# Attention regrouped by head parity, float32 array pieces for scores and fused weights, and a first weight kept whole on the chip

## The chip, the cores and the metric

The kernel runs on one core of one Trainium2 chip. The metric is the device time of one execution in microseconds (us): 1509.26 is the median of three runs before the change (1509.16 to 1510.17). A profile was taken of one execution; its span is 1507.8 us. Engines are named as in the profile: PE is TensorE (products), PEld its weight loads, DVE is VectorE, ACT is ScalarE, POOL is GpSimd, SP is SyncE (which here only issues transfers).

## What is computed

Eight batches of eight heads attend over 576 positions through 32 "packed" queries, and the result goes through two dense layers with a gate, twice (4608 tokens, width 512, inner width 2048).

```python
# q, k, v: (8, 8, 576, 64); p: (8, 8, 32, 64); weights arrive as float64
def sm_attn(qq, kk, vv):
    s = scale * np.matmul(qq, kk.transpose(0, 1, 3, 2))
    a = np.exp(s - np.max(s, axis=-1, keepdims=True))
    a = a / (np.sum(a, axis=-1, keepdims=True) + 1e-09)
    return np.matmul(a, vv)
p_packed = sm_attn(p, k, v)                 # (8, 8, 32, 64)
out = sm_attn(q, p_packed, p_packed)        # (8, 8, 576, 64)
x = out.transpose(0, 2, 1, 3).reshape(4608, 512)
h = x @ w_in;  x = (h * sigmoid(h)) @ w_out                      # first MLP
h = x @ w_in2; x = (h * clip(h + 3, 0, 6) / 6) @ w_out2          # second MLP
```

## The kernel before

**Blocks.** The tokens go through the first MLP in nine blocks of 512. Blocks 0 to 7 are the first 512 positions of batches 0 to 7; block 8 collects the eight tails of 64 positions. In each block (`block`, L1027) a loop over f = 0 to 15 makes 128 hidden rows (`hidden`, L978), applies silu (L1001), splits the result into a high and a low float32r part (`split_g`, L1005) and, two steps later, adds it into four output banks (`project`, L1012). Every product of two values is three float32r products (high x high, high x low, low x high).

**Thin and fat blocks.** Blocks 0 and 8 are fat: `hidden` multiplies all 512 rows of x by the first weight, four chunks x three products. For block 0, x is made by `a_x` (L1674). Blocks 1 to 7 are thin: since x is (softmax weights) x (packed values), the packed values are multiplied into the first weight beforehand (`fuse_steps`, L673), in four groups g of 512 columns, and `hidden` multiplies the fused weight by the softmax weights, two chunks x three products. Batch 1 is fused alone; batches 2 and 3, 4 and 5, 6 and 7 share their products (`mates`, L636). Each product there is three float32r products of 128 rows by 128 columns, 512 wide (L682 to L684), whose operand is loaded from DRAM, where block 0 stored it (`w1i`, `keep`, `next_in`).

**Attention.** Heads are worked on in half batches of four. A score step (`step_zs`, L518) makes, for each pair of heads, one float32 product of 128 rows (two heads of 64, zeros elsewhere) by 64 columns: L528 for the packed queries against k, L524 for q against the packed values, and 64-wide tails (L537, L533). The packed values come from L482 (128 rows by 32 columns, 64 wide). k and q of batches 0 and 1 are turned on PE (L449), later ones on DVE. The k side of a batch runs one block ahead of its q side.

**Order.** All engine queues are in order and the program writes their order by hand. Before block 0 a listed prologue works through batch 0 in two halves. Inside the blocks a planner (`Plan`, L765) puts attention and fusing steps between products: each step has a place in the block, needed steps with a delay counted in products, and a number of PSUM banks, out of a ring of four that `hidden` uses too. A step whose key is "exps" is only run in a calm place (L795). `boundary` (L1942) finishes what the next block needs.

**First weights.** They arrive as pairs of 32-bit words. A unit (`conv_a` to `conv_lo`) is two ACT passes, two DVE passes and a POOL addition (L208), then a cast to the high part on ACT (L219) and a subtraction on DVE (L224). `Feed` (L1449) does two units per f in block 0, loading them on ACT's queue (L155), and stores the results on SP's queue. From block 1 on, `Prep` converts the second MLP's weights with one step per call, and `Second` (L1102) is the second MLP, seven products instead of eight, from block 8's end on.

Of the kernel before, what the change touches and what calls it, by code (L numbers as in the profile page):

```python
# [8 lines left out]
F32 = mybir.dt.float32  # L9
# [9 lines left out]
def tile_pack_attention_two_mlps(ctx: ExitStack, tc, q, k, v, p, w_in1, w_out1, w_in2, w_out2, out):  # L19

# [9 lines left out]
    HQ = P // NP  # L37
    QPB = H // HQ
    NQ = B * QPB
# [5 lines left out]
    RAW = 4  # L45
    assert TAIL * B == T and HQ * D == 2 * P and NP == 32

# [9 lines left out]
    xp = opened(first_left, "xp")  # L57
    gp = opened(first_left, "gp", bufs=3)
    wp = opened(first_right, "wp", side="right")
    at = opened(first_right, "at", side="right")  # L60
    win0 = opened(first_block, "win0", side="right", bufs=3)
# [7 lines left out]
    mask = const.tile([P, HQ, 1], F32, name="mask")  # L69
    nc.vector.memset(mask, 0.0)  # L70
    for h in range(HQ):
        nc.vector.memset(mask[h * NP:(h + 1) * NP, h, :], 1.0)
    twos = const.tile([P, 2, 1], F32, name="twos")
    nc.vector.memset(twos, 0.0)
    for h in range(HQ):
        nc.vector.memset(twos[h * NP:(h + 1) * NP, h % 2, :], 1.0)
    tails = const.tile([P, 2 * TAIL], F32, name="tails")
    nc.vector.memset(tails, 0.0)
    half = const.tile([P, 1], F32, name="half")
    nc.vector.memset(half, 0.5)  # L80
    d1s, d2s = {}, {}
# [8 lines left out]
    early, busy, other = [True], [True], [False]  # L90
    load_queue = [nc.sync]
    banks = [(ps_h, "h"), (ps_h, "h"), (ps_acc, "acc0"), (ps_acc, "acc1"), (ps_h, "h"), (ps_h, "h"), (ps_acc, "acc2")]
    spare = [(wts, f, n) for f in range(0, NF, 2) for n in range(2)] + [(xp, f"xf{c}", 0) for c in range(KC)]
# [10 lines left out]
    def spare_row():  # L104
        return gp.tile([P, 2, T], F32, tag="x1", name="spare", bufs=2).rearrange("p a t -> p (a t)")[:, 0:S]

    def copy(out, in_):
        (nc.vector.tensor_copy if other[0] else nc.scalar.copy)(out=out, in_=in_)

    def copy_short(out, in_):  # L110
        (nc.scalar.copy if busy[0] and not other[0] else nc.vector.tensor_copy)(out=out, in_=in_)

    def vec(step, *args):

        other[0] = True
        step(*args)
        other[0] = False

    def half_kb(n, tag, bufs=1, what=""):

        if n == 1 or (n == 0 and what == "q"):
            pool, tag, n = spare.pop()
            if pool is xp:
                return pool.tile([P, T], F32, tag=tag, name="spare")
            if tag not in shared:
                shared[tag] = pool.tile([P, 2, T], F32, tag=f"wr{tag}", name="spare")
            return shared[tag][:, n]
        return at.tile([P, T], F32, tag=tag, name=tag, bufs=bufs)

# [4 lines left out]
    w1i = [dram.tile([KC, P, 2, GF, P], F32, name=f"w1i{g}", tag=f"w1i{g}") for g in range(NG)]  # L136
# [6 lines left out]
    def half_w(kind, f):  # L143
        if kind == "in":
            return win0.tile([P, 2, DM], F32R, tag="win", name="win")
        if f % 2 == 0:
            return wts.tile([P, 2, DM], F32R, tag=f"wr{f}", name=f"wr{f}")
        return gp.tile([P, 2, DM], F32R, tag="wo", name="wo", bufs=WO)

    def load_raw(key, src):  # L150
        if key[0] == "in":
            raw = wp.tile([P, 2 * T], I32, tag="raw", name="raw", bufs=RAW)
        else:
            raw = win0.tile([P, 2 * T], I32, tag="raw2", name="raw2")
        (load_queue[0] if early[0] else nc.scalar).dma_start(out=raw.rearrange("p (a f) -> p a f", a=src.shape[1]), in_=src)  # L155
        raws[key] = raw
# [7 lines left out]
    def load_win(w, f):  # L164
        load_raw(("in", f), win_src(w, f))

    def load_wout(w, f):
        load_raw(("out", f), wout_src(w, f))


# [3 lines left out]
    def ring():  # L174
        return wp.tile([P, T], F32, tag="ring", name="cr", bufs=8)
# [1822 lines left out]
```

## Time and profile before

| | us |
|---|---|
| median of three runs | 1509.26 |
| span of the profiled execution | 1507.8 |
| PE busy | 1483.1 (98%) |
| DVE busy | 1036.0 (69%) |
| ACT busy | 779.4 (52%) |
| POOL busy | 192.5 (13%) |
| moved by DMA | 358.52 MB, mean 238 GB/s |

The span begins with the program's first instruction and ends with its last; 1.5 us of the median lie around it. Busy time is the union of an engine's instructions. Matmul records overlap (each is shown until its modelled end), so what a product costs is read from the distance between starts, not from its length. A stage is cut out by its start and end in us from the span's start.

### The profile page before, as it was taken

The page shows a single profiled execution, that of the slowest core. Times are in us where ns is not written, and L with a number is a line of the kernel's source. Part 1 is how long each engine was busy: PE and PEld are TensorE (multiplying, and loading weights), DVE is VectorE, ACT ScalarE, POOL GpSimd, SP SyncE. Part 2 cuts the span into 40 slices and gives each one's busy share as a digit, 9 for nine tenths or more (in the row PEclk, how much of TensorE's full clock was granted, in tenths as well). Part 3 has the DMA queues.
Part 4 walks back from the last instruction along what each step waited for, and adds up shares of the span by engine and source line. Part 5 has one row for each costly group of instructions (what it writes and reads, how often), then busy time and mean ns, then how long its engine had stood idle before and what let it go on. Part 6 is the DMA issues. An engine that isn't in the chain of part 4 may idle for free.

```text
span 1507.8 us, 21726 instructions
## 1 busy us (share of the span) xinstructions
PE 1483.1 (98%) x7550; PEld 1230.3 (82%) x7550; DVE 1036.0 (69%) x1695; ACT 779.4 (52%) x1241; POOL 192.5 (13%) x177
## 2 busy tenths in 40 slices
PE   7999999999999999999999999999999999999998
PEld 4777777777777778788878888888888888999998
DVE  6767466756575656653463779786978687778767
ACT  6876657655566456655452344334433443444443
POOL 2433011111211211123240000000000000000000
PEclk9999999999999999999999999999999999999999
DMA  9999789997698769868895576678667866997987
GB/s 246 306 306 276 247 214 253 274 253 198 177 245 263 199 165 306 231 178 239 243 291 178 193 225 216 195 216 252 219 193 223 242 215 210 286 313 255 271 273 226
DMA packets 434509, 358.52 MB, mean 238 GB/s; under 512 B 191200, under 2 KB 325856, under 8 KB 434400
## 3 DMA queue, kind: packets, MB, share of 16 engines
q1 hardware_dynamic: 422832, 343.59, 77.6%
q10 hardware_dynamic: 11568, 13.54, 2.9%
q8 instruction: 61, 1.00, 0.3%
q14 instruction: 48, 0.39, 0.1%
HBM read 295.17 MB, written 61.87 MB: 237 GB/s over the span
## 4 chain that ended last, share of the span: by engine, by line
PE 84%; ACT 6%; DMA 4%; DVE 3%; SPq 2%; issue 1%; POOL 1%; ACTq 0%; POOLq 0%; DVEq 0%
PE b L1270 8%; PE b L1268 8%; PE b L1269 8%; PE b L1363 8%; PE b L1366 7%; PE b L1365 7%; PE acc L1016 7%; PE acc L1017 7%; PE acc L1018 7%; PE hps L992 4%; PE hps L993 4%; PE hps L994 4%; DMA wo<-w1o 1%; DMA praw<-in_moe_w_out_dram 1%; PE abank L524 1%
## 5 line engine op out<-in xcount | busy, mean ns | idle before, releaser
L1009 DVE TENSOR_TENSOR gl<-hps,gh 128x512 fp32r<-128x512 f32 x144 | 98.9, 687 | 190.6 <-ACT gh L1008 187.8
L1366 PE MATMUL b<-ro,ws 128*128 128x512 f32 (+2 forms) x564 | 206.4, 366 | 0.0
L1365 PE MATMUL b<-ro,ws 128*128 128x512 f32 (+2 forms) x564 | 206.3, 366 | 0.0
L1268 PE MATMUL b<-xc,ws 128*128 128x512 f32 (+1 forms) x560 | 205.7, 367 | 0.0
L1270 PE MATMUL b<-xc,ws 128*128 128x512 f32 (+1 forms) x560 | 205.7, 367 | 0.0
L1269 PE MATMUL b<-xc,ws 128*128 128x512 f32 (+1 forms) x560 | 205.7, 367 | 0.0
L1311 DVE TENSOR_TENSOR ro<-g,ro 128x1024 fp32r<-128x1024 f32 (+1 forms) x140 | 161.5, 1158 | 41.5 <-ACT ro L1306 41.2
L1306 ACT CAST ro<-g 128x1024 fp32r<-128x1024 f32 (+1 forms) x140 | 132.0, 967 | 93.4 <-DVE g L1299 34.5
L1001 ACT ACTIVATE hps<-hps 128x512 f32<-128x512 f32 x144 | 83.9, 583 | 116.0 <-PE hps L994 115.0
L1363 PE MATMUL b<-ro,ws 128*128 128x512 f32 (+2 forms) x564 | 138.9, 367 | 0.3
L1366 PEld LDWEIGHTS b<-ro,ws 128*128 128x128 f32 x564 | 105.9, 188 | 13.1
L1365 PEld LDWEIGHTS b<-ro,ws 128*128 128x128 f32 x564 | 105.9, 188 | 13.1
L1268 PEld LDWEIGHTS b<-xc,ws 128*128 128x128 f32 x560 | 105.1, 188 | 13.2
L1269 PEld LDWEIGHTS b<-xc,ws 128*128 128x128 f32 x560 | 105.1, 188 | 13.2
L1016 PE MATMUL acc<-gh,wo 128*128 128x512 f32 x288 | 114.6, 398 | 1.3 <-DMA wo<-w1o 1.3
L1270 PEld LDWEIGHTS b<-xc,ws 128*128 128x128 f32 x560 | 105.1, 188 | 13.0
L1363 PEld LDWEIGHTS b<-ro,ws 128*128 128x128 f32 x564 | 102.9, 188 | 15.0 <-DVE ro L1311 2.1
L1016 PE MATMUL acc<-gh,wr 128*128 128x512 f32 x288 | 114.0, 396 | 0.5 <-ACT gh L1008 0.5
L1017 PE MATMUL acc<-gl,wr 128*128 128x512 f32 x288 | 112.5, 391 | 0.2 <-DVE gl L1009 0.2
L1018 PE MATMUL acc<-gh,wr 128*128 128x512 f32 x288 | 112.5, 390 | 0.0
L1018 PE MATMUL acc<-gh,wo 128*128 128x512 f32 x288 | 112.4, 390 | 0.0
L1017 PE MATMUL acc<-gl,wo 128*128 128x512 f32 x288 | 112.4, 390 | 0.0
(310 smaller groups left out, 2899.4 us busy)
## 6 DMA issues: line engine op xcount, KB each, us to landing
ws<-w2in SPq DMA_DIRECT2D x280, 256.0 KB, 3.3
ws<-w2out SPq DMA_DIRECT2D x280, 256.0 KB, 3.5
wi<-w1i SPq DMA_DIRECT2D x80, 512.0 KB, 6.6
wo<-w1o SPq DMA_DIRECT2D x64, 512.0 KB, 6.2
x1d<-x SPq DMA_DIRECT2D x18, 512.0 KB, 5.2
w1i<-win SPq DMA_DIRECT2D x16, 512.0 KB, 7.2
praw<-in_moe_w_in_dram SPq DMA_DIRECT2D x32, 256.0 KB, 6.2
praw<-in_moe_w_out_dram SPq DMA_DIRECT2D x32, 256.0 KB, 5.7
```

Source lines behind the costliest of these rows:

```text
L1009: nc.vector.tensor_sub(out=gl, in0=g, in1=f32(gh))
L1016: mm(acc[e], lhsT=w[:, 0, s], rhs=gh, start=first, stop=False)
L1017: mm(acc[e], lhsT=w[:, 0, s], rhs=gl, start=False, stop=False)
L1018: mm(acc[e], lhsT=w[:, 1, s], rhs=gh, start=False, stop=last)
L1268: mm(ps, lhsT=wh, rhs=xs[k][:, 0, c], start=first, stop=False, skip_group_check=True)
L1269: mm(ps, lhsT=wh, rhs=xs[k][:, 1, c], start=False, stop=False, skip_group_check=True)
L1270: mm(ps, lhsT=wl, rhs=xs[k][:, 0, c], start=False, stop=last, skip_group_check=True)
L1306: nc.scalar.copy(out=t[:, 0], in_=v)
L1311: nc.vector.tensor_sub(out=t[:, 1], in0=self.operand(s), in1=f32(t[:, 0]))
L1363: mm(to, lhsT=wh, rhs=x, start=False, stop=last, skip_group_check=True)
L1365: mm(to, lhsT=wh, rhs=x, start=first, stop=False, skip_group_check=True)
L1366: mm(to, lhsT=wl, rhs=x, start=False, stop=False, skip_group_check=True)
```

## The change

- A batch is worked on whole. A tile has the four even heads of a batch on one side and the four odd heads on the other: rows e x 64 of a turned tile belong to parity e, and columns c x 32 to head pair c. One softmax tile (`soft`) of 128 x 1152 replaces two of 128 x 576.
- A score step is eight float32 products of 64 rows by 32 columns, 512 wide (`scores_of`), written pair by pair, even then odd; the even ones go to one bank and the odd ones to another. The tails are four products of 128 rows by 32 columns, 128 wide.
- The first weight is converted to plain float32 and kept on the chip (`wi`, four tiles); it is no longer split or stored for fusing. A fusing step is eight such float32 products per group and block (`fuse_products`); its two banks are then split into high and low parts (`fuse_split`). Batches are not paired any more.
- Block 0 is thin too: its g = 0 is fused in the prologue, g = 1 to 3 in the block. `a_x` and its splits go. The prologue works on all eight heads at once and converts four units before block 0.
- Attention of batch j + 1 runs wholly inside block j, with g = 0 of its fusing at 0.88 of the block.
- Block 8's first weight is stored once from `wi` in block 1 (`w1s`), loaded in 16 pieces of 256 KB and split on the chip (`win_load`, `win_split`).
- The planner's class is as it was but for `finish`; the keys of the exponentials are now "exps0", "exps1", "exps20", "exps21".

```diff
-    w1i = [dram.tile([KC, P, 2, GF, P], F32, name=f"w1i{g}", tag=f"w1i{g}") for g in range(NG)]
+    wi = [at.tile([P, KC, T], F32, tag=f"wi{g}", name=f"wi{g}") for g in range(NG)]
+    w1s = [dram.tile([P, KC, GF, P], F32, name=f"w1s{g}", tag=f"w1s{g}") for g in range(NG)]
...
     def conv_add(key):
         r, t = raws.pop(key)
+        if key[0] == "in":
+            nc.gpsimd.tensor_add(out=wi[key[1]][:, key[2], :].bitcast(I32), in0=r, in1=t)
+            return
         nc.gpsimd.tensor_add(out=r, in0=r, in1=t)
...
+    def win_load(f):
+        lo, hi = (fr.tile([P, KC, P], F32R, tag="fused", name="win", bufs=12) for _ in range(2))
+        nc.sync.dma_start(out=f32(lo), in_=w1s[f // GF][:, :, f % GF, :])
+        have_in[f] = hi, lo
+    def win_split(f):
+        hi, lo = have_in[f]
+        nc.scalar.copy(out=hi, in_=f32(lo))
+        nc.vector.tensor_sub(out=lo, in0=f32(lo), in1=f32(hi))
...
+    def scores_of(c, lhs, turned, to):
+        for e in range(2):
+            rows = slice(e * D, (e + 1) * D)
+            mm(to[e][c * NP:(c + 1) * NP, :], lhsT=lhs[rows, c * NP:(c + 1) * NP], rhs=turned[rows, :], start=True, stop=True)
+    def scores_tail(what, lhs):
+        to, dg = bank(), spread_tails[what]
+        for c in range(HP):
+            mm(to[c * NP:(c + 1) * NP, 0:2 * TAIL], lhsT=lhs[:, c * NP:(c + 1) * NP], rhs=dg[:, c].rearrange("p e t -> p (e t)"), start=True, stop=True)
+        return to
...
+    def fuse_products(b, g):
+        to, t = (bank(), bank()), st["ppT", b]
+        for c in range(KC):
+            scores_of(c, t, wi[g][:, c, :], to)
+        return to
+    def fuse_split(b, g, to):
+        made_ = []
+        for e in range(2):
+            hi, lo = (fr.tile([P, T], F32R, tag="fused", name="fused", bufs=12) for _ in range(2))
+            nc.scalar.copy(out=hi, in_=to[e])
+            made_.append((hi, lo))
+        for e, (hi, lo) in enumerate(made_):
+            nc.vector.tensor_sub(out=lo, in0=to[e], in1=f32(hi))
+            fused[b, g, e] = hi, lo
...
+    def attention(b):
+        first = b < 2
+        add("kp", 0.0, 3, lambda: step_small(b), bank=7)
...
+        add("s", 0.17, 6, lambda: step_s(b), ("kp", 7), (last, 7), bank=9, count=3)
...
+        for e in range(2):
+            add(f"max{e}", 0.17, 0, lambda e=e: max1(b, e), ("s", 5 + 3 * e))
+            add(f"exps{e}", 0.17, 0, lambda e=e: exp1(b, e), (f"max{e}", 6))
+        add("t", 0.3, 6, lambda: step_t(b), ("exps1", 10), bank=8, count=3)
+        add("pp", 0.4, 9, lambda: step_pp(b), ("t", 9), ("post1", 0), bank=6)
+        add("pt", 0.45, 3, lambda: step_pt(b), ("pp", 7), bank=7)
+        add("z", 0.52, 6, lambda: step_z(b), ("pt", 8), (last, 7), bank=12, count=3)
...
+        add("m0", 0.88, 4, lambda: fuse(b, 0), ("pt", 9), bank=15, count=2)
...
     def hidden(j, f, tick, nxt):
-        if j in (0, B):
+        if j == B:
...
+    for _ in range(4):
+        feed.load()
...
+    to = fuse_products(0, 0)
+    ub = operand_u(0, 1)
+    fuse_split(0, 0, to)
...
+                plan.add(("m", j, g), lo + (hi - lo) * (0.6 if j else 0.9), 4, lambda g=g: fuse(j, g), bank=15, count=2)
```

## Rows read from the trace of the kernel before

**Rows 1.** The page's first part: busy us, share of the span, instructions

```profile
PE 1483.1 (98%) x7550; PEld 1230.3 (82%) x7550; DVE 1036.0 (69%) x1695; ACT 779.4 (52%) x1241; POOL 192.5 (13%) x177
```

**Rows 2.** Busy time by stage; columns as in the fence's first line

```profile
core 0: us, PE busy (x) PEld busy (x) DVE busy (x) ACT busy (x) POOL busy (x), PEclk, DMA share, GB/s
0.00:36.70 36.70, 27.90 (x196) 17.09 (x197) 22.44 (x58) 22.45 (x44) 8.22 (x15) 0.92 1.01 245
36.70:152.70 116.00, 110.67 (x573) 85.42 (x572) 84.08 (x151) 87.28 (x160) 45.58 (x38) 0.96 0.98 298
152.70:252.00 99.30, 95.69 (x590) 72.45 (x589) 59.10 (x128) 58.62 (x97) 13.84 (x17) 1.00 0.81 220
...
500.00:578.30 78.30, 78.30 (x441) 61.58 (x440) 46.22 (x103) 46.32 (x80) 15.58 (x16) 1.00 0.76 200
578.30:656.80 78.50, 78.49 (x350) 62.37 (x349) 52.62 (x99) 47.79 (x78) 12.02 (x10) 1.00 0.76 225
656.80:722.30 65.50, 65.50 (x291) 54.29 (x290) 28.69 (x57) 35.61 (x62) 21.76 (x18) 1.00 0.84 222
722.30:811.00 88.70, 87.98 (x387) 72.29 (x386) 39.09 (x64) 38.99 (x64) 23.55 (x17) 1.00 0.86 252
```

**Rows 3.** Timeline of PE in block 7: start us, length us, line, tiles, shape

```profile
656.77 0.39 PE L992 MATMUL hps<-a2h,xf 128*128 128x512 f32 x1
...
658.81 0.39 PE L992 MATMUL hps<-a2h,xf 128*128 128x512 f32 x1
```

**Rows 4.** Groups by line, PE, fusing: count, busy us, mean ns

```profile
L682 PE MATMUL abank<-wi,ph 128*128 128x512 f32 x64 | 25.9, 404 | 0.0
```

**Rows 5.** Timeline of PE in block 5, one score step of a half batch

```profile
544.16 1.08 PE L524 MATMUL abank<-T,ppT 128*64 128x512 f32 x4
545.07 1.03 PE L528 MATMUL abank<-T,kp 128*64 128x512 f32 x4
545.93 0.28 PE L533 MATMUL abank<-qtT,ppT 128*64 128x64 f32 x4
...
546.26 0.65 PE L482 MATMUL abank<-nat,T 128*32 128x64 f32 x32
546.84 0.32 PE L485 MATMUL abank<-vt,a1Tt 64*32 64x64 f32 x8
```

**Rows 6.** Timeline of PE in block 0, into and out of a score step

```profile
53.63 0.39 PE L994 MATMUL hps<-xh,win 128*128 128x512 f32 x1
53.95 1.08 PE L528 MATMUL abank<-T,kp 128*64 128x512 f32 x4
...
55.08 0.50 PE L1016 MATMUL acc<-gh,wo 128*128 128x512 f32 x1
55.41 0.40 PE L1017 MATMUL acc<-gl,wo 128*128 128x512 f32 x1
```

**Rows 7.** DMA issues: tiles, queue, count, KB each, median us to landing

```profile
wi<-w1i SPq DMA_DIRECT2D x80, 512.0 KB, 6.6
w1i<-win SPq DMA_DIRECT2D x16, 512.0 KB, 7.2
raw<-in_moe_w_out_dram ACTq DMA_DIRECT2D x13, 512.0 KB, 6.3
```

**Rows 8.** Timeline of ACT's queue in block 0: one issue of a load

```profile
42.01 0.42 ACTq L155 DMA_DIRECT2D raw<-in_moe_w_in_dram  x1
```

**Rows 9.** Groups by line in block 0: count, busy us, mean ns, idle before

```profile
L219 ACT CAST win<-cr 128x512 fp32r<-128x512 f32 x14 | 8.7, 620 | 11.9 <-POOL cr L208 10.6 <-DMA w1i<-win 1.1
L467 ACT ACT_TABLE_LOAD x2 | 2.6, 1283 | 0.0
L224 DVE TENSOR_TENSOR win<-cr,win 128x512 fp32r<-128x512 f32 x14 | 13.7, 980 | 11.1 <-ACT win L219 10.9
L208 POOL TENSOR_TENSOR cr<-cr 128x512 int32<-128x512 int32 x30 | 42.4, 1432 | 61.7 <-DVE cr L199 55.6 <-ACT gh L1008 6.1
```

**Rows 10.** Timeline of DVE in the prologue: a maximum over 576 columns

```profile
22.51 0.75 DVE L1639 TENSOR_REDUCE s2m<-d 128x18 f32<-128x576 f32 x1
```

## What to expect, worked out before the run

> **What bounds the kernel now.** I read the page's busy line first. TensorE (PE) is busy 98% of the span and VectorE (DVE) and ScalarE (ACT) 69% and 52% [rows 1], so the time should come from what PE is given, wherever PE does not wait. To see where that holds I cut the span at the first hidden-layer product of each token block and read the busy time of the stages [rows 2]. A plain block is 16 x 18 = 288 products of 512 columns. Block 7 is almost nothing else: its products start 0.2267 us apart (ten starts, nine steps, in 2.04 us [rows 3]), and 288 x 0.2267 = 65.3 us against its 65.5 us. Everything above 65.5 us in the other thin blocks is therefore attention, fusing or waiting:
>
> - blocks 2 to 6 take 404.8 us together (252.0 to 656.8 [rows 2]), 77.3 us above five plain blocks;
> - block 1 takes 99.3 us, 33.8 above plain;
> - block 0 has 384 products (87.1 us) and takes 116.0 us;
> - the prologue takes 36.7 us.
>
> In block 0 the other engines tell more than PE: ACT is busy 87.3 of 116 us, DMA stands at 0.98 of its 16 engines with 298 GB/s, and PE's granted clock averages 0.96 of 2.4 GHz. There ACT, DVE and DMA set the pace together, not PE alone [rows 2]. The second MLP, from 811 us on, is not touched: 0.
>
> **Block 0's hidden layer.** It goes from 12 to 6 products per f: 96 fewer, 96 x 0.2267 = 21.8 us less PE work.
>
> **Fusing.** Before, blocks 1 to 7 have 192 fused products (three groups of 64 such as the one in [rows 4]), 192 x 0.2267 = 43.5 us: 12 for each pair and group, 48 for block 1 alone. After, each of eight blocks has four steps of eight float32 pieces (64 rows by 32 columns, 512 wide). What such a step costs is the number on which all hangs. The trace shows a pair of float32 pieces of 128 rows by 64 columns: each piece leaves two records, and four records pass in 545.07 - 544.16 = 0.91 us, the next four in 0.86 [rows 5]. It also shows four pieces side by side: 32 records of 128 rows by 32 columns, 64 wide, pass in 546.84 - 546.26 = 0.58 us. Sixteen pieces one after another, at an eighth of 0.86 us each, would be 1.72 us, and still 0.86 if the pieces of a pair ran in turn too. So column groups do run together. No row has two row groups at once. Bounds for a step: 0.86 us (all eight together) and 8 x 0.86 = 6.9 us (one after another), with 1.7 us between if the two row groups take turns. I take 0.91: the eight pieces lie on eight different places of the array, as the four do in the row, their outputs go to two banks, and rows 0 to 63 and rows 64 to 127 read different partitions. The Trainium skill ("TensorEngine Tiling (Array Packing)", sections Tiling Modes and Restrictions and Gotchas) lists 64x32 as eight independent tiles whose row tiles must write different PSUM banks; by that rule the step is near the lower bound, and no run here has shown it yet. The same page says that a change of tiling mode drains the engine, which speaks against many short steps. The rows have that price: the last product before such a step is followed after 53.95 - 53.63 = 0.32 us and the first behind it after 55.41 - 55.08 = 0.33 instead of 0.23 [rows 6], so about 0.2 us, with the drain behind the last piece some 0.3. One fusing step: 0.91 + 0.3 = 1.2 us. Four a block: 4.8 us, and 3.6 in block 7, whose first group is made in block 6.
>
> **Attention on PE, per batch.** Before, block 5 (78.3 us [rows 2]) has 12.8 us above plain; 12 fused products are 2.7, so a batch costs 10.1 us. Of that the change alters three terms. Four pairs of scores, 4 x 0.885 = 3.5 us, become two steps of eight pieces, 2 x 0.91 = 1.8: -1.7. The tail scores, 546.26 - 545.93 = 0.33 us for each half batch [rows 5] and so 0.66, become two sets of four pieces of 128 columns, a quarter of 0.91 and some fill each, 0.5: -0.2. One transpose of p and one of packed values go: -0.2. The packed values (0.58 us for each half in [rows 5]), the turned weights and the tail outputs are as many as before, and so, about, are the entries and exits. After: 8.0 us. Nothing is removed from the softmax itself: its elements are the same, in one tile of 1152 columns instead of two of 576. A steady block is then 65.5 + 8.0 + 4.8 = 78.3, and I add 0.3 for waits of the kind that remain: 78.6. The splits of the fused tiles fall from 16 half-height pairs per block to 8 full-height ones on ACT and DVE, which are busy 46 of 78 us there [rows 2]: hidden, worth nothing by itself. The 80 reads of first weights of 0.5 MB each [rows 7] become 16 of half the size; DMA is at 0.76 in blocks 5 and 6, so this is hidden too.
>
> - Blocks 2 to 6: 5 x 78.6 = 393.0 against 404.8: -11.8.
> - Block 1: 78.6, plus 3 for late loads of the kind it has now; 81.6 against 99.3: -17.7. Its 48 fused products and the half batch that ran ahead go.
> - Block 7: 65.5 + 3.6: +3.6.
> - Block 8: same 384 products. Its 16 first weights are now loaded in one piece and split on the chip, 16 x about 0.6 us on ACT and 0.7 on DVE (a cast and a subtraction of 512 columns), beside 39 us of either in 88.7 us [rows 2]: hidden. Only the first ones stand at the boundary, behind the splits of x: +0.5.
>
> **Block 0.** PE's own sum: 65.5 + 8.0 + 4.8 + 32 transposes of batch 1's k and q (about 4) = 82 us. ACT's sum decides. It has 87.3 us busy now and issues 24 raw loads on its queue (13 in [rows 7], the other 11 of the same kind) at some 0.44 us [rows 8], 10.6 us; the rest of the 116 us is waiting, 10.6 us of it for GpSimd (POOL) in the casts of first-weight tiles alone [rows 9]. The change takes away 14 such casts (8.7 us) and with them that wait, and on DVE the 14 subtractions (13.7 us) [rows 9]. About half the turned k and q tiles go to DVE (-3). It adds six more splits of fused tiles (6 x 0.6 = 3.6) and, I think, two more table loads at 1.28 (2.6 [rows 9]): the planner's rule that an exponential runs only in the calm place behind a silu asks for a step named "exps", and the steps are now "exps0", "exps20" and so on, so exponentials fall where they like. ACT: 87.3 - 8.7 - 3 + 3.6 + 2.6 = 81.8 busy, 26 issues are 11.4, sum 93. With 2 us of waiting 95. ACT's queue is in order, so the product's silu and split stand behind each late cast. PE alone would allow 82; block 0 at its present pace of 116 us is the other end. I take 95: -21. DMA must keep up: 298 GB/s x 116 us = 34.6 MB now; without the 16 stores of first weights of 0.52 MB [rows 7] (8.4 MB) and some five early reads of them (2.6 MB) 23.6 MB are left, 79 us at the same rate. That cover is thin.
>
> **Prologue.** Block 0 now needs all of batch 0, and four converted units, before its first product, where before half a batch after the other could pass. Ahead of the last q piece in the queue are k, v, q (3.5 MB), p and two units of 0.52 MB: 4.6 MB, at 245 GB/s [rows 2] 19 us, plus some 2.5 until data flow: 21.5. Then packing, turning and the scores, 3 us, and DVE's queue: two long and one short piece through transpose, maximum, subtraction, sum and scaling at about 0.7 us each (576 columns take 0.75 [rows 10]), three units' bits at 1.1: 10.7 us, to 35; then two operand transposes and their splits, with the fused split between, 4 us: 39.5. The gain of 12 small products is inside that. Against 36.7: +2.8.
>
> **Sum.** +2.8 - 21.0 - 17.7 - 11.8 + 3.6 + 0.5 = -43.6. The profiled execution's span is 1507.8 us and the median of the runs 1509.26, so 1.5 us lie around the span. 1507.8 - 43.6 + 1.5 = 1465.7, say 1466 us.
>
> **The rivals.** What can be told from no change is about 0.2%, 3 us.
>
> - *The row groups take turns.* Seven batches in blocks have 14 score steps, fusing has 32, the prologue at least 1: 47 steps. If the even and the odd half each run as one group, every step costs 0.86 more: +40 us, 1506. For it: no row shows two row groups together. Against it: the pieces share neither rows, banks nor partitions. 4%.
> - *Slower: every piece waits for the one before.* The pieces are written even head, odd head, next pair, so if row groups exclude each other and PE keeps that order, no two pieces overlap: 47 x 7 x 0.86 = +283 us, 1749. It makes the kernel slower from about 43.6 / 47 = 0.93 us extra per step on, a little over one more turn. 6%.
> - *Block 0 keeps its pace.* ACT, POOL and DVE are chained in order through each converted unit; if POOL's additions (1.43 us each [rows 9]) or DMA set the pace, block 0 stays near 112 to 116 and the prologue ends 3 us later: about 1489. For it: DMA at 0.98 now. Against it: the waits listed are mostly for first-weight casts, which go. 15%.
> - *The softmax chain shows.* A whole batch now runs within one block, with shorter planned delays, three of the four h banks taken at once by a score step, and exponentials with table loads between silus. If PE waits 3 us per block in seven blocks: 1487. 13%.
> - *Block 0 runs at PE's own sum* (82 us): 1453. 10%.
> - *The forecast*, 1466, its own range 1456 to 1478: 52%.
>
> The range 1447 to 1492 holds all but the first two and some tails, about 8 in 10. Faster by over 0.2%: 0.91; within 0.2%: 0.03; slower: 0.06.
>
> **What would show it.** The spacing from the first record of a score or fusing step to the first record behind it: 0.9 to 1.2 us if right, 1.7 or 7 if a rival holds. Block 7 at 69 us is the cleanest place, since it has three fusing steps and nothing else. Block 5 should stay near 78, block 1 stand near 82, block 0 near 95 with ACT close to full and its first product near 39.5 us, and the second MLP should not move. Wrong it would be if blocks 2 to 6 grow (PE idle before steps that follow exponentials), or if block 0's DMA share stays at 0.98 with units arriving late.

## The result, and the profile after

The changed kernel takes 1518.17 us (median of three runs, 1516.45 to 1518.56) against 1509.26: a ratio of 1.0051 with a 95% interval of 1.0031 to 1.0070. It is slower by about 8 us, where 1466 was forecast. The span of its profiled execution, the fastest of the three, is 1514.7 us, 6.9 above that of before. The page's busy line, as [rows 1]: PE is busy 28 us less than before.

```profile
PE 1454.8 (96%) x7860; PEld 1167.6 (77%) x7860; DVE 1011.8 (67%) x1590; ACT 736.0 (49%) x1146; POOL 187.3 (12%) x150
```

Busy time by stage, cut and with columns as in [rows 2]: prologue, blocks 0 and 1, then 3, 6 and 7.

```profile
0.00:43.00 43.00, 26.44 (x204) 12.26 (x204) 22.94 (x48) 16.64 (x31) 7.84 (x13) 0.91 0.84 206
43.00:172.90 129.90, 98.65 (x540) 67.49 (x541) 81.75 (x149) 84.19 (x140) 42.22 (x30) 0.87 0.57 168
172.90:257.70 84.80, 81.41 (x505) 59.05 (x504) 47.09 (x89) 42.33 (x70) 11.77 (x10) 0.98 0.74 209
338.10:417.60 79.50, 79.50 (x505) 58.10 (x504) 47.08 (x93) 43.22 (x72) 13.96 (x12) 1.00 0.64 169
577.80:659.50 81.70, 79.94 (x506) 58.21 (x505) 47.79 (x95) 42.29 (x70) 13.04 (x11) 1.00 0.56 152
659.50:729.50 70.00, 70.00 (x337) 54.33 (x336) 31.11 (x62) 40.09 (x71) 21.84 (x18) 1.00 0.86 234
```

| stage | before | after | forecast of the difference | measured |
|---|---|---|---|---|
| prologue | 36.7 | 43.0 | +2.8 | +6.3 |
| block 0 | 116.0 | 129.9 | -21.0 | +13.9 |
| block 1 | 99.3 | 84.8 | -17.7 | -14.5 |
| blocks 2 to 6 | 404.8 | 401.8 | -11.8 | -3.0 |
| block 7 | 65.5 | 70.0 | +3.6 | +4.5 |
| block 8 | 88.7 | 87.5 | +0.5 | -1.2 |
| second MLP | 696.8 | 697.7 | 0 | +0.9 |

From block 1 on the change gains 13 us. Block 0 and the prologue cost 20. In block 0 ACT is busy about as long as forecast (84.2 us for 81.8) and DVE 81.8 us, DMA has become free (0.57 of its engines against 0.98 in [rows 2]), and yet 130 us pass. What PE waited for in block 0 (waited for, total, times, longest), of before and then of after:

```profile
PE abank L449 <- DVE gl L1009: 4.6, 2, 2.3
PE hps L992 <- DVE gl L1009: 0.6, 1, 0.6
```

```profile
PE abank L567 <- POOL tails L560: 11.0, 1, 11.0
PE acc L829 <- ACT wr L184: 8.0, 1, 8.0
PE hps L802 <- ACT fused L590: 7.3, 3, 3.8
PE abank L406 <- DVE gl L822: 2.6, 1, 2.6
```

Before, PE waits only 5.2 us in all of block 0, but that does not make the other queues slack. The trace's chain (from the last instruction back to what released each one, as far as the profile can infer it) runs through PE for 48 of that block's 116 us. From 37.0 to 74.3 us and from 88.2 to 118.5 it runs through ACT, DVE, POOL and transfers, and PE's two waits of 2.3 us for `gl` stand where these two stretches end. So PE's work and the chain beside it were about equally long. Ends of the second stretch (start us, us, what):

```profile
88.01 0.14 PE abank L537 x4
88.15 1.12 SPq L382
...
117.15 0.59 ACT gh L1008
117.77 0.70 DVE gl L1009
118.51 0.55 PE abank L449 x3
```

After, PE waits over 30 us, and its granted clock averages 0.87 of 2.4 GHz. PE's own sum is about 83.5 us (block 3's 79.5 with no waits, and some 4 for 32 more transposes), so 46 us of block 0 are waits and what follows from them: PE stands for 31 us (129.90 - 98.65), and its work takes some 15 us longer. Part of the 15 is the clock. From 56.1 to 62.9 us, a stretch that begins while PE stands in its wait of 8.0 (51.8 to 59.7 us), the granted clock is 0.50, which is 1.2 GHz, and products start 0.42 us apart (61.19, 61.61); behind it they start 0.23 apart (63.37, 63.60). Some 30 such distances in the block make 7 us; the other 8 were not traced. The stretch by busy time, its clock third from the end:

```profile
56.10:62.90 6.80, 3.16 (x9) 2.45 (x10) 3.83 (x8) 3.78 (x8) 1.07 (x1) 0.50 0.83 291
```

The other queues show where PE's waits begin. DVE's and ACT's longest waits in block 0 of after:

```profile
DVE gl L822 <- ACT gh L821: 34.0, 15, 5.4
```

```profile
ACT cr L142 <- DVE cr L161: 9.9, 7, 2.4
ACT wr L184 <- POOL cr L173: 9.0, 5, 3.8
ACT a2h L540 <- DVE abank L535: 7.9, 2, 4.5
ACT cr L142 <- DMA raw<-in_moe_w_out_dram: 4.5, 2, 4.2
```

DVE stands at `gl` (the low half of a hidden tile) until ACT has made `gh`; ACT stands at a conversion pass or at a cast until DVE's bit passes (L157, L161) or POOL's addition behind them are done. They work in turn rather than side by side. ACT's timeline at the start of the block (start us, us, line, operation, tiles, idle before) shows one such turn, the one behind PE's 8.0:

```profile
46.64 1.28 ACT L510 ACT_TABLE_LOAD   x1
47.94 0.31 ACT L510 ACTIVATE soft<-soft 128x128 f32<-128x128 f32 x1
48.26 1.28 ACT L814 ACT_TABLE_LOAD   x1
...
54.97 0.67 ACT L142 ACTIVATE cr<-raw 128x512 f32<-128x512 f32 x1 [4.21 <-DMA raw<-in_moe_w_out_dram]
...
59.07 0.62 ACT L184 CAST wr<-cr 128x512 fp32r<-128x512 f32 x1 [0.34 <-issue]
```

The cast at 59.07 is second-weight unit 0, for which PE's first output product waits. A table load and an exponential for batch 0's 128 tail columns stand ahead of the block's first silu, and a conversion whose load is late stands ahead of the cast.

### The profile page after: what moved, and what is told of

Same layout as the page of the kernel before. It is cut to its first block, busy times and chain, and to the rows that moved or that the text cites. A ratio compares the mean times of both kernels' runs of the same rounds, so it can differ in the third digit from the quotient of the medians.

```text
span 1514.7 us, 21753 instructions
## 1 busy us (share of the span) xinstructions
PE 1454.8 (96%) x7860; PEld 1167.6 (77%) x7860; DVE 1011.8 (67%) x1590; ACT 736.0 (49%) x1146; POOL 187.3 (12%) x150
## 4 chain that ended last, share of the span: by engine, by line
PE 86%; ACT 5%; DVE 4%; DMA 2%; issue 1%; POOL 1%; SPq 1%; ACTq 0%; POOLq 0%; DVEq 0%
PE acc L829 8%; PE b L1087 8%; PE b L1085 8%; PE b L1086 8%; PE b L1180 8%; PE b L1183 7%; PE acc L831 7%; PE b L1182 7%; PE acc L830 7%; PE hps L802 4%; PE hps L804 4%; PE hps L803 4%; PE abank L406 3%; DMA nat<-in_k_dram 1%; ACT hps L814 1%
## 5 line engine op out<-in xcount | busy, mean ns | idle before, releaser
L829 PE MATMUL acc<-gh,wr 128*128 128x512 f32 x288 | 117.0, 406 | 8.0 <-ACT wr L184 8.0
L829 PE MATMUL acc<-gh,wo 128*128 128x512 f32 x288 | 117.2, 407 | 3.1 <-DMA wo<-w1o 3.0
L802 PE MATMUL hps<-a2h,fused 128*128 128x512 f32 x256 | 107.0, 418 | 7.3 <-ACT fused L590 7.3
L831 PE MATMUL acc<-gh,wo 128*128 128x512 f32 x288 | 114.0, 396 | 0.1
L831 PE MATMUL acc<-gh,wr 128*128 128x512 f32 x288 | 113.5, 394 | 0.4 <-DVE wr L189 0.4
```

What stands on the lines that cost most here:

```text
L802: mm(ps, lhsT=wh, rhs=rh, start=c == 0, stop=False)
L829: mm(acc[e], lhsT=w[:, 0, s], rhs=gh, start=first, stop=False)
L831: mm(acc[e], lhsT=w[:, 1, s], rhs=gh, start=False, stop=last)
```

## Experiments

Block 0 is cut by its first hidden products, as above. The prologue, whose program is the same in most kernels, ends between 42.8 and 45.7 us, so single spans scatter by a few us. Ratios are to the kernel before, on the same chip.

| run | block 0 | ratio (95%) |
|---|---|---|
| changed kernel | 129.9 | 1.0051 (1.0031 to 1.0070) |
| e1_twice | 139.7 | 1.0130 (1.0113 to 1.0146) |
| e2_less_conv | 118.4 | 0.9961 (0.9946 to 0.9976) |
| e3_tails_late | 128.4 | 1.0047 (1.0029 to 1.0065) |
| e4_loads_early | 127.3 | 1.0053 (1.0034 to 1.0072) |
| e5_bits_early | 136.7 | 1.0099 (1.0074 to 1.0124) |
| e6_plan_brisk | 132.1 | 1.0064 (1.0041 to 1.0087) |
| e7_fuse_early | 154.2 | 1.0219 (1.0195 to 1.0243) |
| e8_together | 134.6 | 1.0069 (1.0051 to 1.0087) |
| e9_no_soft | 123.5 | 1.0009 (0.9999 to 1.0019) |
| e10_no_add | 115.8 | 0.9955 (0.9938 to 0.9973) |
| e11_both | 106.0 | 0.9871 (0.9849 to 0.9894) |
| e12_calm | 130.5 | 1.0108 (1.0090 to 1.0126) |
| e13_start | 125.0 | 1.0038 (1.0023 to 1.0053) |
| e14_low_on_pool | 135.4 | 1.0084 (1.0067 to 1.0101) |
| e15_start_pool | 125.3 | 1.0018 (1.0009 to 1.0028) |
| e16_cover | 135.6 | 1.0092 (1.0076 to 1.0107) |
| e17_cover_pool | 140.5 | 1.0111 (1.0093 to 1.0128) |
| e18_bits_ahead | 113.3 | 0.9949 (0.9934 to 0.9963) |

### Is it the PE work that is gone?

```diff
+        if j == 0:
+            for c, (wh, wl, rh, rl) in enumerate(parts):
+                mm(ps, lhsT=wh, rhs=rh, start=c == 0, stop=False)
...
```

> The changed kernel, with each of block 0's 96 hidden-layer products made twice (the second set starts its sum anew, so the values are the same): 96 x 0.2267 = 21.8 us more PE work in block 0, nothing more for any other engine. Theory (the queues of ACT, DVE and POOL set block 0's pace and PE waits for them): block 0 grows by 0 to 8 us, from 129.9 to at most 138, because the products fill waits; the time stays within 1516 to 1526 us. Rival (PE's own work sets the pace): block 0 grows by about 22 us, to 152, and the time to 1540.

It fell between the two: +9.8 us, so over half of the 21.8 us went into waits that were there anyway, and the rest added. More to the point, with PE's load back at 12 products per f block 0 takes 139.7 us where the kernel before takes 116. So the block is not long because PE's cover is gone; the chain beside PE became slower.

### How much of it is load on ACT, DVE and POOL?

Work is left out: conversion passes (`conv_b`, `conv_shift`, `conv_sign` for units converted inside block 0), POOL's additions too, batch 1's softmax passes, and conversion passes and softmax together.

```diff
+        if not early[0] and key[0] != "p":
+            raws[key] = raw[:, :, 1], r, r
+            return
...
-            add(f"exps{e}", 0.17, 0, lambda e=e: exp1(b, e), (f"max{e}", 6))
+            add(f"exps{e}", 0.17, 0, lambda e=e: b == 1 or exp1(b, e), (f"max{e}", 6))
...
```

> The changed kernel, with part of the computation left out: for the units converted inside block 0, one of the two ACT passes (26 of 0.65 us) and both DVE passes (28 units, 0.4 + 0.7 us) are not made; loads, POOL additions, casts and subtractions stay. Theory (the conversion in the in-order queues sets block 0's pace): ACT loses some 15 us and DVE some 28 us of block 0's work, and block 0 falls by 20 to 40 us, to 90 to 110 us. Rival (PE's own work or the float32 pieces set the pace): block 0 stays within 5 us of 129.9. If the loads of raw weights are what is late, it also stays above 120, since they are all still there.

> As the run with fewer conversion passes, and POOL's additions left out too: in block 0 a unit is one ACT pass, then the cast and the subtraction of the second weight; the low bits of these weights are missing. Run with fewer passes: block 0 took 118.4. Theory (what is left there is waits between ACT, DVE and PE over attention and start-up): 108 to 118. Rival (POOL's additions of 1.4 us each, one after another, are the chain's slow link): below 100, near PE's own 82 to 90.

> Block 0 without the softmax passes of batch 1: its maxima, subtractions, exponentials, sums and scalings on DVE and ACT are left out (constants stand in for the first sums), so the numbers of batch 1 are not softmax weights in this run; scores, transposes and conversions stay. It takes some 14 us of DVE and 9 us of ACT (four table loads among them) out of block 0's 130 us. Theory (the conversion of the weights and a whole batch's softmax share the in-order queues, and the late waits come from the sum of both): block 0 falls to 112 to 120, and the 11 us wait before the tail output goes. Rival (the conversion chain alone sets the pace, the softmax fits into its idle time): block 0 stays at 125 or more.

> Both left out in block 0: ACT's second pass and DVE's bit passes of the conversion, and the softmax passes of batch 1. Theory (each of the two fills the queues for the other): block 0 at 95 to 105, about the sum of the two single gains below 130. Rival (PE's own order and the start-up wait set the rest): 110 or more, hardly below the run with fewer conversion passes alone (118.4).

Busy time of block 0 in the run with fewer conversion passes:

```profile
42.80:161.20 118.40, 98.39 (x541) 69.72 (x542) 51.38 (x93) 69.02 (x114) 31.59 (x30) 0.86 0.61 184
```

Taking 30 us of DVE and 15 us of ACT away gives 11.5 us, less than the 20 to 40 expected; the softmax gives 6.4, less than its theory's 10 and more than the rival's 5; both together give 23.9, more than the sum of 17.9 (the 106.0 us lie just above the expected 95 to 105 and below the rival's 110). POOL's additions give 2.6 more, as the theory expected: they are not the slow link. So load counts, but in the first of these runs DVE is busy 51 of 118 us and ACT 69, and PE still waits 7 us for the same first cast and 7 for the same tail step. Engines that are half idle and waits that stay point to order rather than to full queues, which the last run below tests.

### One step at a time

Each of these moves one step and leaves nothing out.

```diff
-        add("xt", 0.8, 2, lambda: step_xt(b), ("ut", 12), bank=6)
+        add("xt", 0.8, 2, lambda: step_xt(b), ("ut", 80 if b == 1 else 12), bank=6)
```

> The changed kernel, with the tail outputs of batch 1 planned later: the product that waits for POOL's masked tails comes 80 instead of 12 units after the transpose it needs, and so falls behind block 0's last products. Theory (the wait of 11.4 us before that product is PE standing at an instruction whose input stands at the end of DVE's backlog): the wait goes and block 0 falls by 8 to 12 us, the time to about 1508. Rival (the backlog holds up the last products anyway, through the gate's split or the turned weights of batch 1): the wait moves to the next product that needs ACT or DVE and the time falls by less than 4 us.

```diff
     conv_begin(unit[5])
+    for _ in range(4):
+        feed.load()
```

> The changed kernel, with four more loads of raw weights issued at the end of the prologue on SP's queue, instead of in block 0 on ACT's queue. Theory (the wait of 8.1 us before the first output product is ACT standing at a unit whose load was issued only 4 us before, with a silu and a cast behind it in the queue): ACT's 4.5 us of waiting for loads go, the wait before the first output product falls from 8 to 2 to 4 us, and the time by 4 to 8 us, to some 1511. Rival (the chain of conversion, with two table loads ahead of it, is late by itself): the wait stays above 6 us and the time within 2 us.

```diff
-    feed.begun, feed.ended, feed.at = 6, 4, 5
+    for key in unit[4:6]:
+        conv_bits(key)
+    for key in unit[4:6]:
+        conv_add(key)
+    feed.begun, feed.ended, feed.at = 6, 4, 6
```

> The changed kernel, with the DVE and POOL passes of the fifth and sixth unit (the first output weight is the sixth) put at the end of the prologue, where DVE then stands idle for 3.5 us, instead of behind the first gate's subtraction. Theory (order, not amount of work: the first output weight is late because its DVE passes stand behind a subtraction that waits for the first silu, which stands behind two table loads and four passes on ACT): the wait before the first output product falls from 8 us to 2 to 4 us and block 0 by 4 to 7 us, to 123 to 126 us, the time to about 1513. Rival (the amount of conversion work is what is late): the work comes back a little later, block 0 falls by less than 2 us.

```diff
-            self.calm, self.slow = False, 1.5
+            self.calm, self.slow = False, 1.0
```

> The changed kernel, with the planner's delays in block 0 taken as they are instead of 1.5 times. Theory (the 11.4 us wait at block 0's end comes from the second softmax of a whole batch being squeezed between the score step at 124 us and the end): the score step comes 8 to 15 us earlier, the softmax is spread over more products, the wait at the end falls from 11.4 us to under 5 us and block 0 by 4 to 10 us. Rival (DVE's queue is full whatever the order): PE meets waits in the middle of the block instead, and block 0 stays within 3 us of 129.9.

```diff
-                plan.add(("m", j, g), lo + (hi - lo) * (0.6 if j else 0.9), 4, lambda g=g: fuse(j, g), bank=15, count=2)
+                plan.add(("m", j, g), lo + (hi - lo) * 0.6, 4, lambda g=g: fuse(j, g), bank=15, count=2)
```

> The changed kernel, with block 0's fusing steps of g = 1 to 3 at 0.6 instead of 0.9 of the group before them. Theory (three waits of 1, 3.4 and 4.2 us come from a fused group being made just before it is used, so that its split on ACT has no cover): these waits fall to under 1 us each where the units are there in time, and block 0 falls by 4 to 8 us. Rival (the units of the first weight are not converted earlier): PE waits for POOL's additions before the fusing step instead, and block 0 changes by less than 2 us.

```diff
-            if key[0] == "exps" and not self.calm:
+            if key[0].startswith("exps") and not self.calm:
...
-            if key[0] == "exps":
+            if key[0].startswith("exps"):
                 self.late = self.now + LATE
```

> The planner's rule for exponentials is given back: every step whose name begins with exps runs only in the calm place behind a silu's split, and delays the banks given out after it. Nothing is left out. Theory (table loads and exponentials in between silus cost little beside the conversion): within 3 us of the changed kernel, 1515 to 1521. Rival (exponentials that fall between a product and its silu hold up PE in block 0 and in blocks 2 to 6, which stand 2 us above what was forecast): 5 to 15 us less, 1503 to 1513.

Late tails: the wait moved, to 7.2 us at the next fusing step, as the rival said. Early loads: ACT's wait for them went and PE's wait for the first cast only fell from 8.0 to 6.7. Brisker plan: nothing, as the rival said. Fusing earlier: PE then waits for the converted first weight itself, and block 0 grows by 24.3 us. The bit passes moved into the prologue: block 0 grows by 6.8, which neither side expected. The calm rule for exponentials made blocks 2 to 5 longer by 1 to 4 us each, so dropping it, as the change does, is a gain; neither side expected that. PE's longest wait in block 0 with fusing earlier:

```profile
PE abank L406 <- POOL wi L171: 21.0, 3, 10.7
```

The run with the bit passes moved had its units begun as late as before but asked for a turn sooner: DVE's wait at `gl` fell to 13.3 us, and waits for casts (17.3 at `wo`, 10.6 at `wr`) took its place; PE waits 17.2 us for fused tiles. Four edits at once (these bit passes, the brisk plan, early fusing, and batch 0's tail piece in the prologue) gave 134.6, as the rival said:

> The changed kernel with the three edits together (passes of two units early, the planner's plain delays in block 0, fusing at 0.6) and the exponential of the first batch's tails moved into the prologue ahead of the silu table, which takes two table loads out of block 0's start. Theory (order): block 0 falls by the sum, 14 to 24 us, to 106 to 116 us, and the time to 1495 to 1505, under the kernel before. Rival (amount of work in the queues): the gains overlap, block 0 stays above 120 us and the time above 1509.

None of these moves made the kernel faster by more than the noise.

### The start, ACT's load, and cover for the fusing step

```diff
     back(2, rest)
+    max2(0, *PIECES[2])
+    sub2(*PIECES[2], nc.vector)
     exp2(*PIECES[1])
+    exp2(*PIECES[2])
...
+    for _ in range(4):
+        feed.load()
...
-            plan.add(("exps3", 0), 0.02, 0, lambda: exp2(*PIECES[2]))
```

> Nothing is left out. The maximum, subtraction and exponential of batch 0's 128 tail columns move from the head of block 0 into the prologue beside the other two pieces (one table load less in block 0), and four raw loads are issued on SP's queue at the end of the prologue instead of on ACT's in the block. Theory (the start-up wait of 8 us is ACT's chain of conversion passes, kdg copy, table load, exponential, table load, first silu): the first output product waits 3 to 5 us instead of 8, block 0 takes 123 to 127, the time is 1508 to 1514. Rival (the wait moves to the next late unit, as with each single step before): block 0 at 128 or more, 1515 to 1520.

```diff
+            nc.gpsimd.tensor_scalar(out=t, in0=raw[:, :, 0].bitcast(U32), scalar1=2.0 ** -29, scalar2=None, op0=ALU.mult)
```

> Nothing is left out: the low word's pass of each conversion in block 0 (26 or so of 0.67 us, 17 us) is done by POOL, which is idle for 88 of 130 us, instead of ACT. Theory (ACT's load in block 0 is part of what makes units and silus late): ACT's busy time falls from 84 to 67 us, POOL's rises from 42 to 65 to 85, block 0 takes 122 to 127. Rival (POOL's longer queue delays the additions, and DVE's two-input passes lengthen beside it): block 0 at 130 to 140.

> Both of these: batch 0's tail piece in the prologue, four loads on SP's queue, and the low word's pass on POOL. If both theories hold, block 0 takes 115 to 122 and the time is 1500 to 1508, at or under that of the kernel before; if either rival holds, it is 1513 or more.

On top of e13_start:

```diff
+            ahead = j == 0 and f >= GF and f % GF == 0
+            if ahead:
+                projects(f - 2, lambda: nxt(f, False))
```

> Nothing is left out. As the run with the moved start, and in block 0 the output products of f - 2 are written ahead of the hidden products of f = 4, 8 and 12, so that six of PE's products lie between each fusing step and the products that wait for its split. Run with the moved start: block 0 125.0, of which 11 to 12 us are waits for fused tiles. Theory (PE's queue is in order, and these waits have nothing of PE's work behind them because of where the steps stand): each of the three is shortened by 1.4 to 2.6 us, block 0 takes 118 to 122, the time is 1507 to 1512. Rival (ACT and DVE hand the same delay on, since the split stands behind conversions whose turn does not come earlier): block 0 at 124 or more, 1513 to 1517.

The start held: PE's wait for the first cast fell from 8.0 to 3.6 us and block 0 by 4.9, as expected. But the time, 1514.7 us, lies just above the interval, and its gain by the ratios, 0.0013 or 2 us, is within the noise. Moving the low pass took 14 us off ACT, and block 0 grew by 5.5, as the rival said: load taken off ACT in this way is no gain, since the pass takes 1.62 us on POOL against 0.67 on ACT. With both, block 0 is as with the start alone, so the two do not add up; the time, 1512.3, lies between what the two sides expected. Covering the fusing step made it worse by 10.6, and the time, 1522.8, is above the rival's range too: DVE's wait at `gl` rose from 31.7 to 44.6 us, which fits hidden products of f = 4, 8 and 12 that come later and hold up all that stands behind `gl` on DVE. With the low pass on POOL as well it was worse still:

> The same, with the low word's pass of the conversions in block 0 on POOL as before in the run of both. That run took 1512.3 with block 0 at 125.3. Theory: 4 to 7 us less, 1505 to 1509, about the kernel before. Rival: 1511 or more.

That pointed at what stands behind `gl`.

### The conversion's bit passes ahead of gl

On top of e13_start, DVE's two passes for a pair of units, and POOL's additions, are written ahead of the `gl` of that f instead of behind it.

```diff
+            if j == 0:
+                feed.bits()
             gs[f] = split_g(g)
...
-            if i < n and i % 2:
-                for step in conv_shift, conv_sign, conv_add:
+        def bits(self):
+            i = self.at
+            if i < len(self.keys) and i % 2 and self.begun > i and self.bitten != i:
+                self.bitten = i
+                for step in conv_shift, conv_sign, conv_add:
```

> Nothing is left out. As the run with the moved start, and in block 0 the two bit passes of two units stand on DVE's queue ahead of the subtraction that makes the low half of the hidden tile (gl) instead of behind it, with POOL's additions; ACT's and PE's queues are as they were. In the changed kernel DVE stands 33.6 us of block 0 at that subtraction, waiting for ACT's cast of the high half (gh), in front of bit passes whose inputs are ready, and ACT then waits 9.9 us for these passes and 5.2 us for POOL's additions behind them. Theory (the loss is engines standing idle in turn in front of ready work): DVE's wait for gh falls below 20 us, units come earlier, block 0 takes 112 to 120 against 125.0, the time is 1502 to 1509. Rival (the queues are full whatever the order, as the runs with other orders seem to say): block 0 at 123 or more, 1512 or more.

DVE in the changed kernel between the second and the third `gl`, then in this run:

```profile
58.77 0.69 DVE L822 TENSOR_TENSOR gl<-hps,gh 128x512 fp32r<-128x512 f32 x1 [5.41 <-ACT gh L821]
59.72 0.69 DVE L189 TENSOR_TENSOR wr<-cr,wr 128x512 fp32r<-128x512 f32 x1 [0.26 <-ACT wr L184]
60.33 0.76 DVE L157 TENSOR_SCALAR cr<-cr 128x512 int32<-128x512 int32 x2
61.00 1.28 DVE L161 SCALAR_TENSOR_TENSOR cr<-raw,cr 128x512 int32<-128x512 int32 x2
...
66.09 0.69 DVE L822 TENSOR_TENSOR gl<-hps,gh 128x512 fp32r<-128x512 f32 x1 [1.26 <-ACT gh L821]
```

```profile
54.03 1.13 DVE L157 TENSOR_SCALAR cr<-cr 128x512 int32<-128x512 int32 x1 [0.28 <-ACT cr L142]
55.09 1.28 DVE L161 SCALAR_TENSOR_TENSOR cr<-raw,cr 128x512 int32<-128x512 int32 x2
56.29 0.68 DVE L822 TENSOR_TENSOR gl<-hps,gh 128x512 fp32r<-128x512 f32 x1
```

Its block 0 by busy time, and its waits of DVE and of PE there:

```profile
45.20:158.50 113.30, 94.63 (x540) 66.11 (x540) 83.45 (x144) 80.81 (x138) 45.87 (x30) 0.91 0.59 174
```

```profile
DVE gl L822 <- ACT gh L821: 6.4, 5, 3.3
```

```profile
PE abank L567 <- POOL tails L560: 5.8, 1, 5.8
PE hps L802 <- ACT fused L590: 4.3, 3, 2.8
PE acc L829 <- ACT wo L184: 4.2, 1, 4.2
```

The theory held; the time is even a little below its range. All work is kept, DVE is even busier (83.5 against 76.4 us in e13_start), and block 0 is 11.7 us shorter than there and 16.6 shorter than in the changed kernel. (As the moved start puts work into the prologue, the end of block 0 is the stricter measure: 172.9 us in the changed kernel, 169.2 in e13_start, 158.5 here.) DVE's wait at `gl` fell from 31.7 to 6.4 us. The pair that DVE makes between 58.77 and 66.09 in the changed kernel stands here ahead of the second `gl`, in time that DVE spent idle. This version takes 1501.0 us (1499.2 to 1503.8, six runs) and beats both kernels, the one before by 0.5%.

## Why the prediction was wrong

**The step that failed** is block 0's, "ACT's sum decides", and in it the 2 us of waiting. PE's own 82 us is borne out by block 3 (79.5) and the transposes, and ACT is busy 84.2 us against 81.8. But ACT is idle for 45.7 us (129.9 - 84.2), where the sum had 13.4 in all, 11.4 for issuing loads and 2 of waiting. That makes 32.3 of the 34.9 us by which the step was off. The four waits of ACT shown above, for DVE's passes, POOL's additions and late loads, make 31.3 of the 45.7 us. Busy time is not pace, and two readings misled.

First, the 2 us had no row behind them. By the forecast's own figures ACT waited 18.1 us of the block before (116 - 87.3 - 10.6), 10.6 of them at the casts that go; the other 7.5 became 2 without a reason, and no new wait was allowed for. The reading that ACT, DVE and DMA set the pace together was half right: PE, which waits 5.2 us, was about as long as they. So PE's 21.8 us could come out only as far as the chain through the other queues got shorter. It got longer, and none came out.

Second, I costed the four first-weight units that now precede block 0 only as a later start. They also push every other unit back. Before, the low half of second-weight unit 0 (`wr`) is made right behind the block's first `gl`, as DVE's timeline there shows; after, behind the second (58.77 and 59.72 above).

```profile
43.74 0.69 DVE L1009 TENSOR_TENSOR gl<-hps,gh 128x512 fp32r<-128x512 f32 x1
44.35 0.68 DVE L224 TENSOR_TENSOR wr<-cr,wr 128x512 fp32r<-128x512 f32 x1
```

In the changed order each engine reaches its wait ahead of work whose inputs are ready. In block 0, 4.9 us came back with the start and 11.7 with the order of the bit passes, together 16.6, a little under half of the 34.9. That the later units are what made this order so dear is read from the timelines and not shown by a run. The kernel before has its bit passes behind `gl` too, and DVE waits only 6.4 us there; and the one run that made two units' bit passes early, e5_bits_early, lengthened the block.

**What stays open** is the rest, 113.3 against 95. The load runs show that 23.9 us can be had by leaving work out, but in the old order, so how much of the 113.3 is load was not measured. The order alone, without the moved start, was not run, nor the kernel before with its bit passes ahead of `gl`.

**Prologue**, +6.3 instead of +2.8: the step was right in kind, but it left out waits. PE waits 5.3 us there for POOL's additions of first-weight units, and DVE's two-input passes run 1.45 and 1.63 us beside POOL instead of 0.69.

**Block 1** came out at 84.8 instead of 81.6, with 3.4 us in which PE is not busy: the 3 us allowed for late loads are what PE waits for a load of `wo`, on top of a steady block that is itself longer.

**Blocks 2 to 6** take 80.4 us instead of 78.6. The mechanism was right: the fusing step, which no row of before showed, takes this long, from its first record to the next product.

```profile
166.64 0.40 PE L831 MATMUL acc<-gh,wr 128*128 128x512 f32 x1
166.97 1.09 PE L406 MATMUL abank<-wi,ppT 64*32 64x512 f32 x16
167.99 0.50 PE L829 MATMUL acc<-gh,wr 128*128 128x512 f32 x1
168.32 0.40 PE L830 MATMUL acc<-gl,wr 128*128 128x512 f32 x1
```

It is 1.02 us: all eight pieces run side by side, and both rivals in which row groups take turns (1.7 and 6.9 us) are refuted. With 0.33 us into it and 0.33 behind it, as in [rows 6], a whole step costs 1.23 us over ordinary products (166.64 to 168.32, less two of 0.2267), for a forecast of 1.2: the number on which all hung was right. The 1.8 us a block lie elsewhere, by the distances between PE's starts: 0.1 in four fusing steps, 0.4 in attention (8.4 us in blocks 3 and 5 for 8.0), some 0.5 in waits beyond the 0.3 allowed, block 6 above all (1.8 us idle), and 0.8 in the ordinary products. These start 0.2305 us apart on average, those beside a step left out, instead of the 0.2267 that the forecast took from block 7; the cause stays open. The Trainium skill ("TensorEngine Tiling (Array Packing)", section Tiling Modes) lists eight independent tiles of 64 by 32; the 1.02 us agree.

**Block 7**, +4.5 for a forecast of +3.6, bears out the price of a step: three at 1.23 make 3.7. The rest is its ordinary products, here too 0.2305 us apart. **Block 8** and the second MLP moved by about 1 us each, as good as forecast.

Of the rivals, "block 0 keeps its pace" was nearest in kind: it had the chain of ACT, POOL and DVE through each unit. The slow links that it named were wrong: leaving POOL's additions out gave 2.6 us, and DMA stood at 0.57. (In number, 1506 for row groups in turn came nearer, by luck: its mechanism is refuted.) "The softmax chain shows" holds in part in block 0, where PE's longest wait, 11.0 us, stands at the end of batch 1's attention and the softmax is worth 6.4 us; in blocks 2 to 6 the same product waits 0 to 1.7 us. Neither sign of being wrong that the prediction named came: blocks 2 to 6 did not grow, and DMA's share fell.

## What to carry to other kernels

Before work is taken from an engine, read two things of the stage: what that engine waits for, and which chain runs beside it through the other queues. An engine that hardly waits can be tied with such a chain, and then the stage gets only as much shorter as the chain does. An engine's busy sum is not that chain: its waits need rows of their own. Where values pass through several in-order queues, a change that puts more of them ahead of the first use must be costed for its effect on the lead of all the others: write down on each queue what stands in front of the ready work. Moving single steps may only move the wait; what helped here was to move the ready work that stood behind the longest wait of an engine that is half idle.

## What the runs showed of the hardware

DVE's passes with two inputs in SBUF lengthen when a two-input pass of POOL has begun before them. DVE in the prologue of the changed kernel, and POOL beside it:

```profile
32.90 1.45 DVE L161 SCALAR_TENSOR_TENSOR cr<-raw,cr 128x512 int32<-128x512 int32 x1
...
39.17 0.69 DVE L161 SCALAR_TENSOR_TENSOR cr<-raw,cr 128x512 int32<-128x512 int32 x1
```

```profile
32.75 1.05 POOL L524 TENSOR_TENSOR soft<-soft,s2s 128x512 f32<-128x512 f32 x1 [7.58 <-DVE s2s L520]
```

The pass that starts at 32.90, 0.15 us behind POOL's, ends at 34.35, some 0.55 after POOL's end at 33.80, as if it had waited for that end. Seven passes of this size in the prologue and block 0 of the changed kernel end so, 0.55 us behind a pass of POOL. The Trainium skill ("SBUF — State Buffer", section SBUF: two separate sides) says that DVE and GpSimd share a port pair as an exclusive lock, also for a DVE operation with two SBUF inputs against a GpSimd one that reads; this row agrees. Rows of e14_low_on_pool do not: there POOL makes the low word's pass, with one input, and DVE's two-input pass beside it keeps its length.

```profile
66.49 0.68 DVE L192 TENSOR_TENSOR wo<-cr,wo 128x512 fp32r<-128x512 f32 x1
```

```profile
65.64 1.53 POOL L151 TENSOR_SCALAR cr<-raw 128x512 int32<-128x512 uint32 x1
```

So that run's loss does not come from longer two-input passes, as its rival had it: the 28 such bit passes of block 0 (L161 in the changed kernel) take 0.68 us on average in both. DVE's one-input bit passes went from 0.42 to 0.54 us, 3.5 us in all, and the low word's pass takes 1.62 us on POOL against 0.67 on ACT.
